# Another order of seven products, an earlier absolute value, and later loads in one stage of an attention and feed-forward kernel

## The chip, the core and the metric

The kernel runs on one core of a Trainium2 chip. A core has five engines with a queue of instructions each: TensorE (PE, with its weight loads shown apart as PEld), VectorE (DVE), ScalarE (ACT), GpSimd (POOL) and SyncE (SP, which here only issues DMA transfers). They run side by side and wait for each other through semaphores. The metric is the device time of one execution in microseconds; times shown are medians of several runs. Positions in the profile are microseconds from the first instruction.

## The reference

Attention with normalised queries and keys is followed by a feed-forward block with a squared ReLU:

```python
# q, k, v: (8, 12, 448, 64); w_in: (768, 2048); w_out: (2048, 768)
def attn(q, k, v, g_q, g_k):
    def rmsnorm(x, g):
        return x / np.sqrt(np.mean(x * x, axis=-1, keepdims=True) + 1e-06) * g
    scores = np.matmul(rmsnorm(q, g_q), rmsnorm(k, g_k).transpose(0, 1, 3, 2)) / 8
    attn = np.exp(scores - np.max(scores, axis=-1, keepdims=True))
    attn = attn / (np.sum(attn, axis=-1, keepdims=True) + 1e-09)
    return np.matmul(attn, v)
# x: the attention's result as (8 * 448, 12 * 64)
h = np.maximum(x @ w_in, 0.0)
out = (h * h) @ w_out
```

q, k, v and the result are float32; the weights w_in and w_out arrive as float64 and are turned into float32 on the chip.

## The kernel before, in words

**Stages.** The eight batches are taken two at a time: four spans of 896 rows. A pair is two heads of one batch; a batch has six pairs, so pairs 0 to 11 belong to span 0, and `NAT` is 12. The kernel first does the attention of span 0 alone (`attention_alone`). Then, for each span, comes the first product with w_in (`first_product`), and then the second product with w_out, whose matmuls are mixed with the attention of the next span. The last span's second product is `last_product`.

**Seven products.** Each matrix product is split into two halves in each direction, and the four block products are made from seven, in the manner of Strassen and Winograd: A11, S2, S1, S3, A12, A22 and S4. The letters name the weight side, for instance A11 a quarter of the weights and S1 a sum of two quarters. The row side has matching matrices: the quarters of x in `xT`, and their differences T1, T2, T3 and T4 in `xC` and `xT`. In `first_product` there are 8 columns `f` of seven products each, so 56 in all; a product is three float32 matmuls of 128 x 128 by 128 x 448, each shown as two records in the profile. The weight side of a product is a tile `sw` of 192 KB, loaded by SP with `load_blocks` from a scratch tensor `w1s` in DRAM. There are five such tiles in turn: a load waits until PE has left the tile of five products ago.

**Banks.** A product is summed in a PSUM bank: A11 and A12 in `pa`, S2 in `pb`, S1 and S4 in `pc`, S3 and A22 in `pd`. The second product in a bank goes on summing onto the first, and may start only once the first has been read: ACT copies A11 to `p1`, and A12 goes on in `pa`; DVE makes `z = p1 + pb`, then `y = z + pc`, and S4 goes on in `pc`; DVE adds `y` and `pd`, and A22 goes on in `pd`. The quarters of the result are then activated by ACT as Relu and Square (in place, L1063 and L1065 of before). `pb`, `pc` and `pd` come from `bank`, which takes two banks, m and n, in turn; `pa` comes from other banks. In the first column of span 0, `order_of` gives the order A11, A12, S2, S1, S3, A22, S4; in all others it is A11, S2, S1, S3, A12, A22, S4.

**Weights.** The float64 weights are turned into float32 while span 0 runs. There are 32 rows of blocks, first 16 of w_in, then 16 of w_out; a row takes one `tick` of four steps in `prepare`, and `weights(upto)` advances the steps. Step 1 has a clamp of the exponents on DVE (L603), step 2 an integer conversion on ACT (L606) and a shift on DVE (L608), step 3 a bit merge on DVE (L613) and, for rows from 13 on, the final integer sum (L579, on DVE) for the row before. The first instruction for a row is the Abs on ACT (`unsigned`, L589), which step 4 issues for the row that comes next, so that step 1 can use it. For each pair of rows, POOL makes four sums (L583), and SP writes the blocks to `w1s` or `w2s`. Rows up to 12 are prepared during `attention_alone`; the rest during the first product of span 0, some 1.76 steps after each product. `u` counts the products from 0.

**What sets the order.** Each engine's queue is the order in which the program issues the instructions; it is written out by hand, and there is no scheduler. [...] At the end of `attention_alone`, for pair 11, SP is given `load(14)` (eight transfers of q and k, into the place where pair 12 lies) and `load_v(12)` (four transfers). The pair 12 is used in the attention that follows this first product; its `transposes` and the `squares` of pair 14 are issued after product 52.

Of the kernel before, what the change touches and what calls it, by code (L numbers as in the profile page):

```python
# [10 lines left out]
F32 = mybir.dt.float32  # L11
U32 = mybir.dt.uint32
AF = mybir.ActivationFunctionType
ALU = mybir.AluOpType
# [373 lines left out]
def attention_then_ffn_bounded(  # L388
# [162 lines left out]
    def prepare(t):  # L551

        def there(n):
            return 0 <= n < 2 * NFC

        def parts(n):
            low, high = pairs_of(words_of(n))
            return exponents_of(n), exponents_of(n).bitcast(U32), low, high  # L560

        def value(n, half):
            if not there(n):
                return

            to = ((A11, A12), (A21, A22)) if n < NFC else ((A11, A21), (A12, A22))
            places = [place_of(n, k) for k in to[n % 2]]
            part = slice(half * HW, (half + 1) * HW)
            if not doubles:
                nc.gpsimd.tensor_copy(blocks_of(n)[:, places[half]], words_of(n).bitcast(F32)[:, part])  # L570
                return
            _, eu, low, _ = parts(n)
            if n < EARLY // 4:
                dst = blocks_of(n)[:, places[half]]
                nc.gpsimd.tensor_tensor(*[x.bitcast(I32) for x in (dst, low[:, part], eu[:, part])], ALU.add)
            elif half == 0:
                dst = blocks_of(n)[:, places[0]:places[1] + 1:places[1] - places[0]]
                low, eu = (x.rearrange("p (h m) -> p h m", h=2) for x in (low, eu))
                nc.vector.tensor_tensor(*[x.bitcast(I32) for x in (dst, low, eu)], ALU.add)  # L579

        def total(n, dst, x, y, op):
            if there(n) and n % 2:
                nc.gpsimd.tensor_tensor(*[blocks_of(n)[:, place_of(n, i)] for i in (dst, x, y)], op)  # L583

        def unsigned(n):

            if there(n) and doubles:
                e, _, _, high = parts(n)
                nc.scalar.activation(e, high.bitcast(F32), AF.Abs)  # L589

        if t == 0:
            unsigned(0)
        n = t - 3
        if there(n) and n % 2:
            c = n % NFC // 2
            dst = w1s[c] if n < NFC else w2s[:, c // 4, :, c % 4]
            first = place_of(n, A11)
            nc.sync.dma_start(dst.rearrange("k p m -> p k m"), blocks_of(n)[:, first:first + 7])
            written[0] = n + 1
        if there(t) and doubles:  # L600
            e, eu, low, high = parts(t)

            nc.vector.tensor_scalar(e, e, 2.0 ** -15, 1.875 * 2.0 ** 16, ALU.max, ALU.min)  # L603
        yield
        if there(t) and doubles:
            nc.scalar.activation(low.bitcast(I32), low, AF.Copy, scale=2.0 ** -29)  # L606
            bits = banks.get("bits", eu)
            nc.vector.tensor_scalar(bits, eu, 3, 0x3FFFFFF8, ALU.logical_shift_left, ALU.bitwise_and)  # L608
        if t < 3:
            load_words(t, t - 1)  # L610
        yield
        if there(t) and doubles:
            nc.vector.scalar_tensor_tensor(eu, high, 0xC0000000, bits, ALU.bitwise_and, ALU.bitwise_or)  # L613
        total(t - 2, S3, A11, A21, ALU.subtract)
        total(t - 2, S4, A12, S2, ALU.subtract)
        value(t - 1, 0)
        yield
        unsigned(t + 1)
        value(t - 1, 1)
        total(t - 1, S1, A21, A22, ALU.add)  # L620
        total(t - 1, S2, S1, A11, ALU.subtract)
        load_words(t, t - 1)
        yield
# [17 lines left out]

    def order_of(span, f):

        return (A11, A12, S2, S1, S3, A22, S4) if span == f == 0 else range(7)

    N1 = HF * 7
    FIRST = (5,5,5)
# [288 lines left out]
    def attention_alone():  # L936


        for i in range(NAT):
            more = i + 1 < NAT  # L940
            if 0 < i < NAT - 3:
                load(i + 3)
            scores(i, 0)
            scores(i, 1)
            if i == 0:

                transpose(1, 1, 1)
                scores(0, 2)
                scores(0, 3)
                transpose(1, 0, 0)  # L950
                add_up(0, 1)
                norm(2)
                load_v(1)
                values(0, (0, 1))
                load(3)
                yield
                continue
            if more:
                transpose(i + 1, 1, 0)
            values(i - 1, (2, 3))  # L960
            add_up(i, 1)
            if i + 2 < NAT:
                norm(i + 2)
            elif not more:
                norm(NAT)
                load(NAT + 2)
            yield
            if more:
                transpose(i + 1, 0, 0)
            load_v(i + 1)  # L970
            if i + 2 < NAT:
                roots(i + 2)
            yield
            scores(i, 2)
            scores(i, 3)
            total_of(i - 1)
            values(i, (0, 1))
            finish(i - 1)
            yield
            if added(i) == 3:  # L980
                add_up(i, 2)
            combine_x(i - 1)
            if NAT <= i + 3 < NAT + 2:
                load(i + 3)
            yield
        values(i, (2, 3))
        total_of(i)
        finish(i)
        combine_x(i)
# [67 lines left out]
    def first_product(work, span):  # L1057
# [10 lines left out]

        for f in range(HF):
            n = begins[span, 1] + f * 7  # L1070
            order = order_of(span, f)
            g11, g12 = gT[:, f, 0:S], gT[:, f, S:2 * S]
            g21, g22 = gT[:, HF + f, 0:S], gT[:, HF + f, S:2 * S]
            add = nc.vector.tensor_tensor
            ps_of = {}
            for at, i in enumerate(order):

                into, rhs = {A11: ("pa", B11), S2: ("pb", T2), S1: ("pc", T1), S3: ("pd", T3),
                             A12: ("pa", B21), A22: ("pd", T4), S4: ("pc", B22)}[i]
                first = into not in ps_of  # L1080
                if first and into == "pa":
                    if span == 0 and f:
                        ps_of[into] = ps_o.tile([P, S], F32, tag="ot"[f % 2], name="pa")
                    else:
                        ps_of[into] = ps_s.tile([P, 2, 512], F32, tag="s", name="pa")[:, 0, 0:S]
                elif first:
                    ps_of[into] = bank(into)
                ps = ps_of[into]
                load_blocks(n + at + 5)
                for c in range(HC):  # L1090
                    nc.tensor.matmul(ps, stream[n + at][:, c], rhs[:, c], start=first and c == 0,  # L1091
                                     stop=c == HC - 1, skip_group_check=not first)
                if i == A11:
                    p1 = work.tile([P, S], F32, tag="p1", name="p1", bufs=1)
                    nc.scalar.copy(p1, ps)  # L1095
                elif i == S2:
                    z = work.tile([P, S], F32, tag="z", name="z")
                    add(z, p1, ps, ALU.add)  # L1098
                elif i == S1:
                    y = work.tile([P, S], F32, tag="y", name="y")  # L1100
                    add(y, z, ps, ALU.add)
                elif i == A12:
                    activate(g11, ps)
                else:
                    g, x = {S3: (g22, y), A22: (g21, z), S4: (g12, z)}[i]
                    add(g, x, ps, ALU.add)  # L1106
                    activate(g, g)
                if span and f and i in (S1, A22):
                    combine(f - 1, (int(i == A22),))
                if span and f == HF - 1 and i == S4 and span + 1 < NSPAN:  # L1110
                    combine(f)
                yield
# [359 lines left out]
    with tc.tile_pool(name="words", bufs=2) as spare["pool"]:  # L1472
# [20 lines left out]
        with tc.tile_pool(name="first_product", bufs=2, reuse_waits="tile") as work:  # L1493
            for u, _ in enumerate(first_product(work, 0)):
                if u == 6:

                    left = ps_s.tile([P, 2, 512], F32, tag="s", name="bits")
                    banks["bits"] = left.rearrange("p a b -> p (a b)")[:, 0:NW].bitcast(U32)
                weights(min(ALL, EARLY + (ALL - EARLY) * (u - 1) // (N1 - 6)))
                if u == N1 - 5:  # L1500
                    norm(NAT + 1)
                if u == N1 - 4:
                    transposes(NAT)
                    squares(NAT + 2)
# [124 lines left out]
```

## Time and profile before

| what | us |
|---|---|
| median of three runs | 1347.29 (1347.04 to 1348.31) |
| the profiled execution, in all | 1347.79 |
| its span, first to last instruction | 1346.0 |
| PE busy | 1324.7 |
| attention alone | 0 to 133.14 |
| first product of span 0 | 133.14 to 263.94 |
| the rest | 263.94 to 1346.0 |

The granted clock of TensorE was 0.999 of full speed. In the profile, `L1091` is line 1091 of the kernel before. A row "A <- B" of the waits says that A's engine stood still until B released it, with the total time, the number of times and the longest. A row of the timeline gives start, length, engine, line and operation, what it writes and reads, and in brackets the idle time ahead of it. The chain that ended last follows the last instruction back through whatever released each step.

### The profile page before, as it was taken

Reading aid. Unit: us, or ns where it says so; the run is one execution under the profiler, and the core shown is the slowest. Engines: PE = TensorE matmul, PEld = TensorE weight load, DVE = VectorE, ACT = ScalarE, POOL = GpSimd, SP = SyncE. Lnnn points to the kernel's source line nnn. Section 1 sums busy time; section 2 is a strip of 40 time slices with the busy share of each in tenths; the row PEclk is TensorE's granted clock in tenths of the full one; section 3 lists DMA queues with packets and bytes.
Section 4 is the critical chain, followed back from the end, with each engine's and each line's share of the span. In section 5 each row is a group of like instructions: output and inputs, shape, how many; then the busy total and the mean of one; then the engine's idle time right before and its main releaser. Section 6 shows DMA issues by size and latency. Waiting matters only on the chain.

```text
span 1346.0 us, 17761 instructions
## 1 busy us (share of the span) xinstructions
PE 1324.7 (98%) x5930; PEld 698.9 (52%) x5930; DVE 861.9 (64%) x1333; ACT 486.4 (36%) x939; POOL 681.0 (51%) x546
## 2 busy tenths in 40 slices
PE   8999999999999999999999999999999999999997
PEld 3333444444445655444444755444444665556887
DVE  6999788489988233467888533457888823336553
ACT  7886466555541011345553011235554101111000
POOL 5766533466765222647774522447676522322452
PEclk9999999999999999999999999999999999999999
DMA  8977999666665433346755433345664444421333
GB/s 226 244 214 200 312 357 331 187 131 121 138 140 125 104 88 88 102 105 132 149 125 144 110 90 88 92 113 117 134 129 128 107 100 139 131 88 47 115 103 56
DMA packets 413817, 190.18 MB, mean 141 GB/s; under 512 B 282388, under 2 KB 408724, under 8 KB 413716
## 3 DMA queue, kind: packets, MB, share of 16 engines
q1 hardware_dynamic: 406164, 180.21, 51.8%
q0 software_dynamic: 4736, 8.40, 2.5%
q8 instruction: 49, 0.80, 0.3%
q10 hardware_dynamic: 2816, 0.34, 0.2%
q14 instruction: 52, 0.43, 0.1%
HBM read 155.72 MB, written 33.16 MB: 140 GB/s over the span
## 4 chain that ended last, share of the span: by engine, by line
PE 87%; DVE 7%; ACT 4%; issue 1%; DMA 1%; POOL 0%; SPq 0%; DVEq 0%; ACTq 0%
PE ps L1190 21%; PE pd L1091 11%; PE pa L1091 10%; PE pc L1091 10%; PE sc L796 7%; PE pav L878 7%; PE pb L1091 5%; PE ps L1373 3%; PE ps L1241 2%; PE pd L1345 2%; PE pc L1345 2%; PE pa L1345 2%; ACT gT L808 2%; PE pd L1175 1%; PE pc L1175 1%
## 5 line engine op out<-in xcount | busy, mean ns | idle before, releaser
L1067 POOL TENSOR_TENSOR gT<-gT 128x448 f32<-128x448 f32 x96 | 94.2, 983 | 258.0 <-ACT gT L1063 258.0
L761 POOL TENSOR_TENSOR half<-half,mhalf 128x28 f32<-128x28 f32 x36 | 184.1, 5115 | 70.2 <-DVE half L760 56.2
L1190 PE MATMUL ps<-gT,sw 128*128 128x448 f32 x432 | 169.3, 545 | 0.0
L1063 ACT ACTIVATE gT<-gT 128x448 f32<-128x448 f32 x96 | 55.4, 577 | 300.5 <-DVE gT L1106 300.5
L1091 PE MATMUL pa<-xT,sw 128*128 128x448 f32 x384 | 155.0, 540 | 0.6 <-ACT p L1095 0.6
L1190 PEld LDWEIGHTS ps<-gT,sw 128*128 128x128 f32 x432 | 80.1, 190 | 87.2 <-issue 85.2
L1190 PE MATMUL ps<-gC,sw 128*128 128x448 f32 x288 | 113.1, 546 | 0.0
L796 PE MATMUL sc<-qkT 64*64 64x448 f32 (+1 forms) x1152 | 110.1, 497 | 0.3 <-ACT pr L798 0.2
L1091 PEld LDWEIGHTS pa<-xT,sw 128*128 128x128 f32 x384 | 72.7, 190 | 71.8 <-issue 70.5
L583 POOL TENSOR_TENSOR gC<-gC 128x384 f32<-128x384 f32 x64 | 76.4, 1213 | 63.4 <-DVE gC L579 61.7
L1190 PEld LDWEIGHTS ps<-gC,sw 128*128 128x128 f32 x288 | 53.2, 190 | 59.5 <-issue 57.7
L846 POOL DMA_DIRECT2D xT<-factors x72 | 38.1, 534 | 89.9 <-DMA factors<-square 65.2
L1106 DVE TENSOR_TENSOR gT<-z,pd 128x448 f32<-128x448 f32 x32 | 19.8, 620 | 97.8 <-PE pd L1091 97.8
L798 ACT ACTIVATE pr<-sc 128x896 f32<-128x896 f32 x87 | 76.9, 909 | 11.1 <-PE sc L796 11.1
L1091 PE MATMUL pd<-xT,sw 128*128 128x448 f32 x192 | 77.9, 542 | 1.5 <-DVE z L1098 1.4
L763 POOL TENSOR_TENSOR qk<-qk,half 128x448 f32<-128x448 f32 x72 | 76.9, 1089 | 2.8
L1091 PE MATMUL pd<-xC,sw 128*128 128x448 f32 x192 | 77.5, 540 | 0.7 <-DVE gT L1106 0.7
L1091 PE MATMUL pb<-xC,sw 128*128 128x448 f32 x192 | 77.5, 540 | 0.2 <-DVE gT L1106 0.2
L1091 PE MATMUL pc<-xT,sw 128*128 128x448 f32 x192 | 77.5, 540 | 0.0
L1091 PE MATMUL pc<-xC,sw 128*128 128x448 f32 x192 | 77.4, 539 | 0.0
L878 PE MATMUL rest<-pr,vt 64*64 64x448 f32 x348 | 72.7, 537 | 0.0
L878 PE MATMUL pav<-pr,vt 64*64 64x448 f32 x348 | 72.7, 537 | 0.0
(282 smaller groups left out, 2455.1 us busy)
## 6 DMA issues: line engine op xcount, KB each, us to landing
sw<-w1s SPq DMA_DIRECT2D x224, 192.0 KB, 2.4
sw<-w2s SPq DMA_DIRECT2D x102, 256.0 KB, 3.5
w1s<-gC SPq DMA_DIRECT2D x8, 1344.0 KB, 6.9
w2s<-gC SPq DMA_DIRECT2D x8, 1344.0 KB, 6.8
qk<-in_q_dram SPq DMA_DIRECT2D x144, 56.0 KB, 2.6
qk<-in_k_dram SPq DMA_DIRECT2D x144, 56.0 KB, 2.4
xT<-factors POOLq DMA_DIRECT2D x72, 112.0 KB, 3.4
vt<-in_v_dram SPq DMA_DIRECT2D x72, 96.0 KB, 3.8
```

Source lines behind the costliest of these rows:

```text
L583: nc.gpsimd.tensor_tensor(*[blocks_of(n)[:, place_of(n, i)] for i in (dst, x, y)], op)
L761: nc.gpsimd.tensor_tensor(half, half, mhalf, ALU.pow)
L763: nc.gpsimd.tensor_tensor(qkn[:, s], raw[:, s], half[:, s * NG:(s + 1) * NG].rearrange("p g -> p g ()").to_broadcast([P, NG, 32]), ALU.mult)
L796: nc.tensor.matmul(sc[part, h, 0:n], qkT[rows, 0, 1, keys], qkT[rows, 0, 0, of], start=True, stop=True)
L798: nc.scalar.activation(pr, sc[:, :, 0:n], AF.Exp)
L878: nc.tensor.matmul(into, vs[i][rows, h, c, :], probs[i, c][rows, h, :], start=(c == 0), stop=(c == NF), skip_group_check=True)
L1063: nc.scalar.activation(g, src, AF.Relu)
L1067: nc.gpsimd.tensor_tensor(g, g, g, ALU.mult)
L1091: nc.tensor.matmul(ps, stream[n + at][:, c], rhs[:, c], start=first and c == 0, stop=c == HC - 1, skip_group_check=not first)
L1190: nc.tensor.matmul(ps, stream[n][:, c % 4], rhs_of[i][:, c], start=c == 0, stop=c == HF - 1)
L1345: nc.tensor.matmul(ps, lhs[:, c], rhs[:, c], start=first and c == 0, stop=c == HK - 1, skip_group_check=not first)
L1373: nc.tensor.matmul(ps, weights_of(o, m, c // HK)[:, c % HK], rhs_of[i][:, c, part], start=c == 0, stop=c == HF - 1)
```

## The change

Three things change, all in or around the first product of span 0.

1. The first column of span 0 takes the products in the order A11, S1, A12, S2, S3, S4, A22. `y` is made as soon as both `pb` and `pc` are there. In this column, `pb` takes the bank that held the even pairs' values, `pc` is bank m and `pd` bank n; one extra turn keeps the alternation of the later columns as it was.
2. The Abs of the next row is issued in step 3, before its end, instead of step 4, for ticks from 13 on.
3. `load(14)` and `load_v(12)` leave the end of `attention_alone` and are issued, the v first, after product 40 of the first product.

```diff
         value(t - 1, 0)
+        if t >= EARLY // 4:
+            unsigned(t + 1)
         yield
-        unsigned(t + 1)
+        if t < EARLY // 4:
+            unsigned(t + 1)
         value(t - 1, 1)
...
-        return (A11, A12, S2, S1, S3, A22, S4) if span == f == 0 else range(7)
+        return (A11, S1, A12, S2, S3, S4, A22) if span == f == 0 else range(7)
...
                 norm(NAT)
-                load(NAT + 2)
...
-            load_v(i + 1)
+            if more:
+                load_v(i + 1)
...
             n = begins[span, 1] + f * 7
+            turn[0] += span == f == 0
...
+                elif first and span == f == 0:
+                    ps_of[into] = (ps_o.tile([P, S], F32, tag="o", name="pb") if into == "pb"
+                                   else bank(into, int(into == "pd")))
                 elif first:
                     ps_of[into] = bank(into)
...
-                elif i == S2:
-                    z = work.tile([P, S], F32, tag="z", name="z")
-                    add(z, p1, ps, ALU.add)
-                elif i == S1:
-                    y = work.tile([P, S], F32, tag="y", name="y")
-                    add(y, z, ps, ALU.add)
+                elif i in (S2, S1):
+                    if i == S2:
+                        z = work.tile([P, S], F32, tag="z", name="z")
+                        add(z, p1, ps, ALU.add)
+                    if "pb" in ps_of and "pc" in ps_of:
+                        y = work.tile([P, S], F32, tag="y", name="y")
+                        add(y, z, ps_of["pc"], ALU.add)
...
                 weights(min(ALL, EARLY + (ALL - EARLY) * (u - 1) // (N1 - 6)))
+                if u == 5 * N1 // 7:
+                    load_v(NAT)
+                    load(NAT + 2)
```

## The prediction

> **What bounds the kernel now.** I read the page first: the busy times and the engines' shares of the chain that ended last.
>
> ```profile
> PE 1324.7 (98%) x5930; PEld 698.9 (52%) x5930; DVE 861.9 (64%) x1333; ACT 486.4 (36%) x939; POOL 681.0 (51%) x546
> PE 87%; DVE 7%; ACT 4%; issue 1%; DMA 1%; POOL 0%; SPq 0%; DVEq 0%; ACTq 0%
> ```
>
> PE is the bound, idle for 1346.0 - 1324.7 = 21.3 us. Only idle time of PE in the stage that the change touches can be won. The view by stretches (attention alone, span 0's first product, the rest) puts it in size:
>
> ```profile
> 0.00:133.14 133.14, 124.06 (x611) 47.89 (x611) 115.84 (x179) 104.15 (x186) 86.41 (x70) 1.00 0.82 224
> 133.14:263.94 130.80, 127.95 (x341) 63.29 (x344) 97.47 (x127) 71.53 (x114) 57.98 (x53) 1.00 0.88 302
> 263.94:1346.00 1082.06, 1072.66 (x4984) 587.72 (x4984) 648.61 (x1027) 310.73 (x639) 536.57 (x425) 1.00 0.47 112
> ```
>
> The columns are length, busy time of PE, PEld, DVE, ACT and POOL, clock, DMA share, GB/s. The middle stage is the one changed: PE idles 2.85 us, and its DMA share is 0.88. PE's timeline there has one row per product of six matmul records:
>
> ```profile
> 133.14 2.52 PE L1091 MATMUL pa<-xT,sw 128*128 128x448 f32 x6
> 136.28 2.52 PE L1091 MATMUL pa<-xT,sw 128*128 128x448 f32 x6 [0.62 <-ACT p L1095]
> ...
> 146.28 2.52 PE L1091 MATMUL pd<-xC,sw 128*128 128x448 f32 x6 [0.71 <-DVE gT L1106]
> ...
> 169.26 2.52 PE L1091 MATMUL pb<-xC,sw 128*128 128x448 f32 x6 [0.16 <-DVE gT L1106]
> ...
> 191.35 2.52 PE L1091 MATMUL pd<-xT,sw 128*128 128x448 f32 x6 [1.35 <-DVE z L1098]
> ...
> 261.52 2.42 PE L1091 MATMUL pc<-xT,sw 128*128 128x448 f32 x6
> ```
>
> Undisturbed products start every 2.2555 us (138.64, 140.90, 143.15). Fifty-five such steps are 124.05 us, but the first and last starts lie 128.38 us apart: 4.33 us are lost, the refill of about 0.1 us after each stall included. By starts: 0.99 at product 1, 0.98 at product 5, 0.42 at 15, 0.17 at 18, 1.62 at 24, 0.15 at 41. The waits of this stretch say what makes DVE late:
>
> ```profile
> DVE gC L603 <- ACT gC L589: 14.1, 8, 2.1
> PEld pc L1091 <- DMA sw<-w1s: 0.6, 1, 0.6
> ```
>
> L589 is the Abs of a row. DVE's timeline shows the wait ahead of the 1.35 us stall:
>
> ```profile
> 184.28 0.61 DVE L1106 TENSOR_TENSOR gT<-z,pc 128x448 f32<-128x448 f32 x1
> 186.94 0.97 DVE L603 TENSOR_SCALAR gC<-gC 128x768 f32<-128x768 f32 x1 [2.05 <-ACT gC L589]
> ...
> 190.68 0.61 DVE L1098 TENSOR_TENSOR z<-p,pb 128x448 f32<-128x448 f32 x1
> ```
>
> After its addition of 184.28, DVE sits 2.05 us, because ACT first does Relu and Square of that sum and only then the Abs. SyncE's timeline at the stage's start shows the transfers that move:
>
> ```profile
> 133.88 1.89 SPq L688 DMA_DIRECT2D qk<-in_q_dram  x4
> 135.87 2.00 SPq L688 DMA_DIRECT2D qk<-in_k_dram  x4
> 137.91 0.48 SPq L543 DMA_DIRECT2D gT<-in_moe_w_out_dram  x1
> 138.48 0.92 SPq L705 DMA_DIRECT2D vt<-in_v_dram  x2
> 139.44 1.33 SPq L707 DMA_DIRECT2D vt<-in_v_dram  x2
> ```
>
> **What the skill says.** The Trainium skill, "TensorE: Matmul & The Clock Gate" (opening table), gives ScalarE, VectorE and GpSimd strict first-in-first-out queues; the 2.05 us above is such a queue. "DMA: Bandwidth & Descriptors" (Anatomy of one DMA) says a DMA's semaphore wait happens on the issuing sequencer; the trace agrees, as the loads above begin only when POOL's scaling of pair 12 is done, and the weight tiles wait behind them until 140.87. The same page (Specifications) wants 512 B or more per piece for full rate; q and k go in packets of 128 B, and DMA shows 0.35, 0.69 and 0.96 busy at only 57 to 111 GB/s over 134 to 140 us. "SBUF — State Buffer" (Who interferes with whom) says a DVE operation with two SBUF inputs contends with GpSimd; xC's subtractions took 1.30 us beside POOL and 0.62 without.
>
> **The change part by part.** No instruction is added or taken away; they are only reordered.
>
> *Order of products.* Product k would start at 133.14 + 2.2555k. Product 1 is now S1 into bank pc: its operand T1 is many microseconds old, so nothing waits, and the copy of A11 (135.70 to 136.24) hides under it; A12 at 137.65 finds it done. A product is released 2.46 us after its start (143.15 to 145.61). S2 starts at 139.90; its operand's last part was ready at 138.5. Then DVE: z at 142.4 to 143.0, y (which now needs z) to about 143.8; S4, which adds onto the bank that y reads, starts at 144.42, margin 0.6. S3 is released at 144.62. DVE has two row operations first (0.55 + 0.96), so the sum of S3 ends near 145.8; A22 needs that bank at 146.67, margin 0.9. Thus both stalls go: -1.97 us. If DVE were later by more than these margins, the excess comes back one for one.
>
> *Banks.* Column 1's pb and pc now wait for S4's and A22's sums, two and three products old, where pb had one product's time before. Afterwards the alternation is the same. Zero.
>
> *Abs one step earlier.* In ACT's order each Abs now stands ahead of Relu and Square, which wait for DVE. Its own waits, for a row's words and for POOL's value sums of four rows back, ended earlier (POOL's last is at 143.94). Its 0.9 us delays one Relu; readers of that are a stage away. It frees up to 14.1 us of DVE. At product 15: the sum of A22 can start at its release, 133.14 + 12 x 2.2555 + 2.46 = 162.67; the four operations to the end of S4's sum took 165.34 to 169.20, so 166.53, against 166.97 when product 15 wants the bank: margin 0.44. At product 24: A22's sum at 178.45, S4's sum begins 3.27 later (181.01 to 184.28), row work 0.53 after, z ends 4.36 after that (186.94 to 191.30): 186.61 against 187.27, margin 0.66. Gain -0.42 - 0.17 - 1.62 = -2.2 us. The loss of 0.15 at product 41 is a weight tile behind a w2s write that waits for POOL, which waits for DVE; that goes too, while tile 18, behind such a write, may now cost about 0.1.
>
> *The loads moved.* At the start, four v and eight q/k issues leave the queue (3.99 + 2.29 = 6.28 us). A row of w_out and the weight tiles from 5 on go out when the product ahead frees their buffer. Nothing to win by itself, but tile 9, which took 8.9 us, gets room. The 12 issues now come after tile 44's, at product 39's release, 133.14 + 39 x 2.2555 + 2.46 = 223.6; 0.3 for tile 44, then 6.28: tile 45 issues at 230.2 and is wanted at 234.6. Landing took 2.3 at least, 5.2 in the median, 8.9 at most: 232.5 to 239.1. Next in the queue is a w2s write, then tile 46, wanted at 236.9 and likely landing at 235 to 237.5. Row 30's value sum on DVE waits for that write's landing (6.8 median: 237.5, against the 237.4 at which DVE gets there); behind it is the sum of S3, which A22 needs with some 0.4 to spare. So the cost lies between 0 and about 4 us. I take 0.7, as DMA was only 0.64 and 0.46 busy at 228 to 232 before. Squares of pair 14, which need the data, come twelve products later and are covered.
>
> Sum: -4.33 + 0.1 + 0.7 = -3.5 us. All later work follows the products and is PE-bound (0.20 and 0.31 are its longest PE gaps), so the gain stays. The profiled execution had 1346.0 us of span and 1347.79 in all; the median of the runs is 1347.29, so I forecast 1347.29 - 3.5 = 1343.8, with a span near 1342.5. A measurement of this kernel tells about 0.2% (2.7 us) from no change.
>
> **Rivals.**
> *A: all stalls go, with a small wait near product 45.* 1342.9 to 1344.6, chance 0.66.
> *B: only the new order pays.* DVE runs at 97.47 of 130.80 us, and the margins of 0.44 and 0.66 may be eaten by POOL's port, or words may come late; then the later stalls stay or tiles 45 and 46 eat 2 us: 1347.29 - 1.97 = 1345.3. Against it: eight Abs waits are gone for two margins that need one. Chance 0.21.
> *C: slower.* The 12 small transfers meet a busy DMA, each of the later ones waits for the eighth before it to land, and two rounds of 8.9 us pass: tile 45 issues at 241.7, lands near 245, and PE stands 10 us: 1347.29 - 4.3 + 10 = 1353. It decides once tile 45 lands 4.3 us after 234.6, at 239, and is measurable from 241.6. Against it: the same burst took 6.28 us before. Chance 0.11.
> *D: the moved Abs does nothing,* as ACT is still held by a wait in front of it: as B's time. Chance 0.02.
>
> **Numbers.** Predicted 1343.8 (A). The range 1342.6 to 1347.0 takes in A and B, the 4.33 us won in full, and half of the doubtful cost of the burst. Faster by over 0.2% (below 1344.6): 0.67; within: 0.22; slower: 0.11.
>
> **What would show it.** Right: products 1 and 5 start without idle time; DVE's row of waits on Abs falls from 14.1 to under 4 us; the last product starts near 258 instead of 261.52; the later stage keeps its 1082 us. Wrong: PE or its weight load waits on a weight tile or on a sum between 230 and 245 for more than 1 us; or DVE still late at products 15 and 24.

## The result and the profile after

The changed kernel took 1345.03 us in the median of 22 runs (1343.33 to 1346.61), the kernel before 1347.26 us in 22 runs beside them (1345.68 to 1349.32). The ratio is 0.9983, with a 95% interval of 0.9977 to 0.9988: 2.2 us less, between 1.6 and 3.1. The profiled execution has a span of 1343.1 us instead of 1346.0.

The page's busy row and the three stretches of the kernel after (length, then busy time of PE, PEld, DVE, ACT and POOL, clock, DMA share, GB/s):

```profile
PE 1324.0 (99%) x5930; PEld 699.4 (52%) x5930; DVE 860.5 (64%) x1333; ACT 486.2 (36%) x939; POOL 681.1 (51%) x546
```

```profile
0.00:133.23 133.23, 124.38 (x610) 47.83 (x610) 116.50 (x179) 104.01 (x186) 86.23 (x70) 1.00 0.82 225
133.23:261.20 127.97, 127.25 (x337) 63.51 (x337) 98.74 (x127) 71.51 (x114) 57.62 (x52) 1.00 0.88 307
261.20:1343.10 1081.90, 1072.34 (x4985) 588.05 (x4984) 645.23 (x1027) 310.64 (x639) 537.22 (x426) 1.00 0.47 112
```

The changed stage is 127.97 us long instead of 130.80, and PE is idle in it for 0.72 us instead of 2.85. The other two stretches kept their length within 0.2 us. PE's timeline of the kernel after, one row per product:

```profile
135.59 2.42 PE L1098 MATMUL pc<-xC,sw 128*128 128x448 f32 x6
...
146.87 2.42 PE L1098 MATMUL pd<-xC,sw 128*128 128x448 f32 x6
...
167.16 2.42 PE L1098 MATMUL pb<-xC,sw 128*128 128x448 f32 x6
...
187.69 2.52 PE L1098 MATMUL pd<-xT,sw 128*128 128x448 f32 x6
...
226.44 2.52 PE L1098 MATMUL pc<-xT,sw 128*128 128x448 f32 x6 [0.15 <-DMA sw<-w1s]
...
238.48 2.49 PE L1098 MATMUL pa<-xT,sw 128*128 128x448 f32 x6 [0.50 <-DMA sw<-w1s]
...
258.85 2.42 PE L1098 MATMUL pc<-xT,sw 128*128 128x448 f32 x6
```

The rows shown are products 1, 6, 15, 24, 41, 46 and 55. Product 0 starts at 133.23; its 55 successors, at 2.2555 us each, would take 124.05 us, and they take 125.62. I call the difference the stage's loss: 1.57 us, where the kernel before lost 4.33. The stalls at products 1, 5, 15 and 18 are gone, but for 0.10 us at product 1, which every profile with the new order shows. What is left besides is 0.33 at product 24, 0.41 at 41 and 0.73 at 46. Two of these rows name weight tiles as the reason. In the kernel before no row of PE named one, but two of its small losses were waits for tiles as well: tile 18 landed at 176.09, and PE began product 18 at 176.23; tile 41 landed at 229.80, and PE began product 41 at 229.84. The waits of 130 to 265 us after:

```profile
DVE gC L603 <- ACT gC L589: 0.7, 2, 0.3
...
PEld pc L1098 <- DMA sw<-w1s: 0.9, 1, 0.9
...
PE pa L1098 <- DMA sw<-w1s: 0.5, 1, 0.5
```

DVE's wait on Abs fell from 14.1 us to 0.7.

### The profile page after: what moved, and what is told of

Read it like the earlier page. It is cut to its first block, busy times and chain, and to the rows that moved or that the text cites. A ratio compares the mean times of both kernels' runs of the same rounds, so it can differ in the third digit from the quotient of the medians.

```text
span 1343.1 us, 17769 instructions
## 1 busy us (share of the span) xinstructions
PE 1324.0 (99%) x5930; PEld 699.4 (52%) x5930; DVE 860.5 (64%) x1333; ACT 486.2 (36%) x939; POOL 681.1 (51%) x546
## 4 chain that ended last, share of the span: by engine, by line
PE 86%; DVE 7%; ACT 3%; DMA 3%; issue 1%; POOL 0%; SPq 0%; DVEq 0%; ACTq 0%; POOLq 0%
PE ps L1198 21%; PE pd L1098 10%; PE pa L1098 10%; PE pc L1098 10%; PE sc L799 7%; PE pav L881 7%; PE pb L1098 5%; PE ps L1381 3%; PE ps L1249 2%; PE pd L1353 2%; PE pc L1353 2%; PE pa L1353 2%; PE pd L1183 1%; PE pc L1183 1%; DMA sw<-w1s 1%
```

## The experiments

The table has every combination of the three parts, and the later variants. The loss is from one profile each; the ratio of the times to the kernel before has its 95% interval.

| kernel | stage's loss, us | where most of it is (product: us) | ratio |
|---|---|---|---|
| before | 4.33, again 4.30 | 1: 0.99, 5: 0.98, 24: 1.62 | 1 |
| e1 order | 3.56 | 9: 1.03, 15: 0.76, 24: 1.61 | 0.9994 (0.9986 to 1.0003) |
| e2 Abs | 2.72 | 1: 0.99, 5: 0.97, 18: 0.43 | 0.9991 (0.9984 to 0.9997) |
| e3 loads | 6.10 | 1, 5: 1.97, 18: 0.59, 24: 1.61, 46: 1.51 | 1.0015 (1.0007 to 1.0023) |
| e5 order, Abs | 0.87 | 9: 0.46, 24: 0.33 | 0.9982 (0.9975 to 0.9989) |
| e6 order, loads | 5.51 | 10: 0.80, 15: 1.07, 24: 1.62, 46: 1.94 | 1.0007 (0.9998 to 1.0016) |
| e10 Abs, loads | 3.71 | 1, 5: 1.97, 41: 0.41, 46: 0.74 | no interval |
| all three | 1.57, again 1.63 (e8) | 24: 0.33, 41: 0.41 and 0, 46: 0.73 and 1.22 | 0.9983; e8 0.9982 (0.9974 to 0.9990) |
| e4, e9 all, loads spread | 0.68, again 1.12 | 9: 0.26 and 0, 24: 0.33, 41: 0 and 0.71 | 0.9976 (0.9967 to 0.9985); e9 0.9976 (0.9965 to 0.9986) |

### e1: the new order alone

```diff
-        return (A11, A12, S2, S1, S3, A22, S4) if span == f == 0 else range(7)
+        return (A11, S1, A12, S2, S3, S4, A22) if span == f == 0 else range(7)
```

with the banks and `y` as in the change.

> The kernel before with the new order of products in span 0's first column alone; Abs and loads stay as before. Theory (the parts are separate): products 1 and 5 lose nothing (1.97 us back), products 15, 18 and 24 still lose about 2.2 us because DVE still waits about 14 us for Abs; first to last product start 126.4 us instead of 128.4, time 2 us lower. Rival (DVE paces the stage, so that what PE wins early it gives back at products 15 and 24): products 15 and 24 lose about 4 us, first to last stays near 128.4 and the time is within 0.5 us of before.

First to last took 127.61 us: between the two, and the time can't be told from that of the kernel before. Products 1 and 5 lose only the 0.10 us named above, and the waits on Abs stayed (14.0 us). But a new stall ate half of the gain, at product 9:

```profile
154.45 2.49 PE L1095 MATMUL pc<-xC,sw 128*128 128x448 f32 x6 [0.79 <-DMA sw<-w1s]
```

Its weight tile was issued at 144.60 and landed at 154.32, 9.7 us later. A weight row (143.10) and a w1s write of 1344 KB (143.58) were issued just ahead of it. With the early stalls gone, product 9 also comes sooner after that issue: its turn was 8.9 us later, where the kernel before had 9.8. (A product's turn is the start of the product before it plus 2.2555 us.) The theory that each part stands alone fell with this run. DVE as the pace of the stage could explain only the growth of product 15's loss from 0.42 to 0.76.

### e2: the earlier Abs alone

```diff
+        if t >= EARLY // 4:
+            unsigned(t + 1)
         yield
-        unsigned(t + 1)
+        if t < EARLY // 4:
+            unsigned(t + 1)
```

> The kernel before with the Abs one step earlier alone. Theory: DVE's wait on Abs falls from 14.1 us to under 3, products 15, 18 and 24 lose about 0.4 us together instead of 2.2, products 1 and 5 still lose 1.97; first to last near 126.5 us, time 1.8 us lower. Rival (the order is needed for the Abs to come in time): DVE keeps over 8 us of waits on Abs and first to last stays over 127.5 us.

```profile
DVE gC L603 <- ACT gC L589: 0.7, 2, 0.3
```

First to last took 126.77 us, and the ratio of 0.9991 is 1.2 us. Product 15 lost nothing and product 24 lost 0.33. Product 18 lost 0.43, but not because of DVE: its weight tile landed 8.69 us after its issue, and PE waited for it. The two are more than the 0.4 expected for them together. The Abs comes in time without the new order; the rival fell.

### e3: the moved loads alone

```diff
                 norm(NAT)
-                load(NAT + 2)
...
-            load_v(i + 1)
+            if more:
+                load_v(i + 1)
...
+                if u == 5 * N1 // 7:
+                    load_v(NAT)
+                    load(NAT + 2)
```

> The kernel before with the load of pair 14's q and k and of pair 12's v moved to product 40 alone. Theory (the move costs and gives nothing by itself): a weight tile is late by about 0.7 us near product 46, the other losses stay at about 4.2 us; first to last near 129.0 us, time 0.5 to 0.8 us higher. Rival (the move gives: the weight tiles and rows at the stage's start come earlier and DVE is less late): products 15 to 24 lose 1 us less and the time is lower by 0.5 us or more.

```profile
242.67 2.49 PE L1091 MATMUL pa<-xT,sw 128*128 128x448 f32 x6 [1.28 <-DMA sw<-w1s]
```

The move is a loss of its own: 1.51 us at product 46 instead of 0.7, the stalls on DVE and ACT untouched, 0.59 us at product 18 for a late weight tile, the ratio 1.0015, about 2 us. In this kernel DVE's value sum of row 30 also stood 0.5 us for a w2s write to land.

### e5 and e6: two parts together, without loads and without Abs

Each is the changed kernel with one part put back: in e5 the loads of e3's diff, in e6 the Abs of e2's diff.

> The changed kernel with the twelve loads back at the end of the attention: order and Abs alone. Theory (in the order alone tile 9 came 0.95 us late because the burst of loads at 134 to 140 us pushed the weight rows and the w1s write together in front of it): product 9 is late again by 0.7 to 1.2 us, nothing is lost at product 46, and the stage loses 1.5 to 2.2 us in all (the changed kernel 1.57). Rival (tile 9's lateness came from DVE's lateness, through the w1s write): product 9 loses under 0.3 us and the stage under 1.1 us.

e5 lost 0.87 us in all. Product 9 was late by 0.46: between theory and rival, with the stage's loss on the rival's side. Whether DVE's lateness had a part in e1's 1.03 is not shown: the step from 1.03 to 0.46 is no larger than what tile 9's landing time moves by (7.6 to 8.9 us in the six profiles that have the new order and the loads moved). Nothing was lost at product 46. The stage loses 0.7 us less than the changed kernel does; the two ratios, 0.9982 and 0.9983, can't be told apart.

> The changed kernel with the Abs back in step 4: order and loads alone. Theory: product 9 is in time, products 15 and 24 lose about 2.2 us as DVE waits about 14 us for Abs, and product 46 loses about 1.4 us, as with the loads alone, since a late DVE makes the w2s write come in the middle of the burst; in all about 3.7 us and a time 0.5 us lower than before. Rival (0.7 us at product 46 are the burst's own, whatever DVE does): 0.7 us at product 46, in all about 3.0.

e6 was worse than both expected: 5.51 us. Product 9 was in time, as expected. With the new order, it lost 1.03 and 0.46 us where the loads stand at the start (e1, e5), and where they are moved it lost nothing in five of six profiles and 0.26 in e4; so moving the loads does ease that delay. But then the late DVE showed one product later, ahead of product 10:

```profile
153.36 0.95 DVE L603 TENSOR_SCALAR gC<-gC 128x768 f32<-128x768 f32 x1 [2.06 <-ACT gC L589]
```

```profile
155.88 2.52 PE L1095 MATMUL pd<-xT,sw 128*128 128x448 f32 x6 [0.53 <-DVE z L1103]
...
241.72 1.74 PE L1095 MATMUL pa<-xT,sw 128*128 128x448 f32 x4 [1.70 <-DMA sw<-w1s]
```

The last row is product 46, with 1.94 us lost. The two kernels with the loads in one burst and the late Abs (e3 and e6) lost 1.51 and 1.94 there, the ones with the early Abs 0.73, 1.22 and 0.74. The chain through product 46 has the tile from issue to landing, first in the changed kernel, then in e6:

```profile
232.16 6.18 DMA sw<-w1s
```

```profile
235.30 6.28 DMA sw<-w1s
```

In all five profiles with the burst the tile took about the same time, 6.15 to 6.28 us. What differs is how long before the product's turn it was issued: 5.7 us in the changed kernel and in e10, where the 0.41 us lost at product 41 had put off that turn, 5.2 in e8, 4.9 in e3 and 4.6 in e6. In e3 and e6 the burst took longer, since its first two transfers (v) held the queue for 1.35 and 1.65 us, and for 0.96 in the others. Why these two issues took longer is open.

### e10 and e11: the last combination, and the kernel before again

> The last of the eight combinations: Abs and loads without the new order. Theory (the burst costs 0.7 us in the stage when DVE is early and nearly 2 us when it is late): 1.97 us lost at products 1 and 5, about 0.4 at 18 and 24, 0.7 to 1.2 at product 46, in all 3.0 to 3.8 us. Rival (the burst's cost depends on the order of products instead): nearly 2 us at product 46, in all over 4.2 us.

e10, the kernel before with e2's and e3's diffs together, lost 3.71 us, 0.74 of it at product 46 and 0.41 at product 41: as the theory had it.

> The kernel before, profiled again, for how far a stage's loss moves from profile to profile: 4.1 to 4.6 us at the same products if the losses are fixed by the order of instructions; over 0.5 us away if they are chance.

e11 lost 4.30 us. The stalls on DVE and ACT repeat within 0.02 us. The stalls on weight tiles do not: product 18 lost 0.32 instead of 0.17, and product 41 nothing instead of 0.15. In the changed kernel and its repetition e8, product 41 lost 0.41 and 0, and product 46 lost 0.73 and 1.22. These two belong together, since a loss at product 41 puts off the turn of product 46: their sums are 1.14 and 1.22.

### e4, e8 and e9: the loads spread over three products

```diff
-                if u == 5 * N1 // 7:
+                if u == 39:
                     load_v(NAT)
-                    load(NAT + 2)
+                if u in (42, 46):
+                    load(NAT + 2, (u == 46,))
```

where `load` is given which of q and k it is to load.

> The changed kernel with the twelve loads issued in three groups of four, v after product 39, q after 42 and k after 46, instead of all twelve after product 40. Theory (SyncE's queue holds tile 45 and 46 back for the 6.7 us of the burst): the loss of 0.73 us at product 46 goes to under 0.1, first to last 0.6 us shorter than in the changed kernel (125.6), near 125.0 us. Rival (the w2s write ahead of tile 46 and a busy DMA delay it, not the queue): a loss of 0.4 us or more stays between products 42 and 50.

In the changed kernel, SyncE's queue around product 40 was this (start, length, line, what):

```profile
224.44 0.96 SPq L708 DMA_DIRECT2D vt<-in_v_dram  x2
...
226.82 2.16 SPq L691 DMA_DIRECT2D qk<-in_q_dram  x4
229.02 2.04 SPq L691 DMA_DIRECT2D qk<-in_k_dram  x4
...
231.69 0.38 SPq L598 DMA_DIRECT2D w2s<-gC  x1
232.16 3.92 SPq L672 DMA_DIRECT2D sw<-w1s  x4
```

The burst holds the queue from 224.44 to 231.06. The w2s write then goes out at 231.69, just ahead of tile 46 at 232.16, which lands at 238.35, while product 46 wanted it at 237.82. In e4 the write leaves earlier and the tile follows at 228.12:

```profile
225.03 1.18 SPq L672 DMA_DIRECT2D sw<-w1s  x2
226.76 0.37 SPq L598 DMA_DIRECT2D w2s<-gC  x1
228.12 0.32 SPq L672 DMA_DIRECT2D sw<-w1s  x1
```

```profile
236.95 2.42 PE L1099 MATMUL pa<-xT,sw 128*128 128x448 f32 x6
```

That is product 46, without a wait. First to last was 124.74 us, and product 46 lost nothing, neither here nor in the repetition e9. Its tile went out 8.8 us ahead of its turn, as it does in e5, which has no burst there, and not 5.7 us. So the burst in front of it was the cause of that loss. The w2s write stands just ahead of the tile in e4 as well, so the write alone does not make it late; what the write adds to the landing time was not tested (tile 45, issued before the write, landed after 2.9 us, and tile 46, behind it, after 6.2).

> The changed kernel as it is, beside the one with the spread loads. Theory: the stage loses 1.2 to 1.8 us, ratio to before near 0.9983.

> The spread loads again, beside the changed kernel. Theory: the stage loses 0.5 to 1.0 us, 0.7 us less than the changed kernel, and its ratio to before is 0.0004 to 0.0007 lower. Rival (the difference seen between them was chance): the same ratio within 0.0002.

Side by side, the changed kernel lost 1.63 us and the spread one 1.12 us, 0.71 of that at product 41 with a tile that took 9.0 us to land. That is 0.5 us less, where the theory had 0.7, and more than the 0.5 to 1.0 it gave the spread loads. The ratios are 0.9982 and 0.9976, so the spread one is 0.0006 lower; e4 had 0.9976 too. The intervals overlap, so its lead over the changed kernel is shown by the profile's product 46 and not by the times.

### e7: without POOL's sums beside DVE

```diff
-            if there(n) and n % 2:
+            if there(n) and n % 2 and n != 19:
```

in `total` of e4's kernel.

> The kernel with the spread loads, without POOL's four sums for the weight rows 18 and 19, whose blocks S1 to S4 are then left unset, so that the part of the result that uses them is not the reference's. Theory (DVE's value sum at 185.4 took 1.72 us instead of 0.95 because POOL's sums ran beside it): that sum takes 0.95 us again and product 24 loses nothing (0.33 us before). Rival (it was late for another reason): product 24 loses 0.2 us or more.

The changed kernel ahead of product 24, DVE and then POOL:

```profile
182.44 1.05 DVE L603 TENSOR_SCALAR gC<-gC 128x768 f32<-128x768 f32 x1
...
184.51 0.95 DVE L613 SCALAR_TENSOR_TENSOR gC<-gC,bits 128x768 uint32<-128x768 uint32 x1
185.39 1.72 DVE L579 CUSTOM_DVE_ANT_0 gC<-words,gC 128x1536 uint16<-128x1536 uint16 x1
187.03 0.61 DVE L1106 TENSOR_TENSOR z<-p,pb 128x448 f32<-128x448 f32 x1
```

```profile
182.07 4.22 POOL L583 TENSOR_TENSOR gC<-gC 128x384 f32<-128x384 f32 x4 [5.75 <-DVE gC L579]
```

and e7 (one run):

```profile
181.96 0.55 DVE L603 TENSOR_SCALAR gC<-gC 128x768 f32<-128x768 f32 x1
...
184.42 0.95 DVE L579 CUSTOM_DVE_ANT_0 gC<-words,gC 128x1536 uint16<-128x1536 uint16 x1
185.28 0.61 DVE L1107 TENSOR_TENSOR z<-p,pb 128x448 f32<-128x448 f32 x1
```

Without POOL's four sums the value sum takes 0.95 us again, z starts 52.52 us after product 0 instead of 53.80, and product 24 loses nothing. This confirms the theory, and shows that it was not the value sum alone: the clamp of L603 takes 0.55 us instead of 1.05. The two make up nearly all of the 1.28 us. In the kernel before the same POOL sums ran from 184.44 to 188.77, while DVE was waiting for Abs or in other operations, and the value sum came at 189.81, after them.

## Why the prediction was right, and where its sum was off

**Right: the order of products.** Products 1 to 8 run without a gap. The steps came where they were laid: z at 142.63, y from 143.28 to 143.90, the sum of S3 ending at 145.99, A22 at 146.87. Of the 1.97 us, the 0.10 at product 1 stays. What was laid as a separate gain is one only together with the other parts: alone it gave 0.77 us (e1), and 2.14 (3.71 to 1.57) when the other two are there.

**Right: the Abs.** The wait fell from 14.1 to 0.7 us, and S4's sum ahead of product 15 ended at 166.73, where 166.53 was laid, against a start at 167.16. This is the largest part: 1.61 us alone, and 3.94 us (5.51 to 1.57) when the other two are there.

**Right by luck: product 18.** The prediction put its 0.17 us to the Abs, though it also laid 0.1 for a late tile there. But product 18 waited for its weight tile, and it lost 0.17 to 0.59 us in all five profiles of the old order, with the early Abs too (0.43 in e2, 0.26 in e10), and nothing in the eight of the new order. So it is the order that ended this stall. How is open: the tile was issued 8.4 to 8.5 us ahead of its turn in all of them.

**Off: product 24.** The term read "z ends 4.36 after that", from a row in which DVE's value sum had POOL quiet beside it. With the wait gone, DVE reaches that sum inside POOL's stretch, and it takes 1.72 us instead of 0.95: z ended at 187.64, not 186.61. Of the 1.03 us between, 0.77 is the value sum, 0.08 the clamp (1.05 us instead of the 0.97 of the row that was used), and the rest, 0.19, moved product 24's turn as well. So a margin of 0.66 met 0.85 us that was not in the sum. The prediction quoted the sentence of the Trainium skill, "SBUF — State Buffer" (Who interferes with whom), that a DVE operation with two SBUF inputs contends with GpSimd, and named this as a threat to the margin, but put no number on it. Cost: 0.33 us, the refill of 0.10 included.

**Wrong: product 41.** "That goes too" did not hold: the changed kernel lost 0.41 us there. Tile 41 did go out earlier, 8.4 us ahead of its product's turn instead of 7.8, but it took 8.72 us to land, where it had taken 7.83. In e8 it was issued at the same place, landed after 8.07 us, and nothing was lost; in e9 it took 9.0 us and cost 0.71. What sets the landing time is not shown. In 11 of the 13 profiles the tile landed 0.3 to 0.6 us after the w2s write of 1344 KB that was issued just ahead of it.

**Right in mechanism, low in size: the loads.** The queue was held for 6.6 us, where 6.28 was laid; tile 45 issued at 231.16 (230.2 laid) and was in time; tile 46 behind the w2s write was late by 0.73, where the allowance for all was 0.7. That these two agree is luck: 0.7 was picked from a span of 0 to 4 us, and the loss at product 41 had put off the turn of product 46. Without it, e8 shows 1.22. One of the prediction's own signs of being wrong, a wait of PE or its weight load for more than 1 us between 230 and 245, was met by the weight load of product 46:

```profile
238.45 0.30 PEld L1098 LDWEIGHTS pa<-xT,sw 128*128 128x128 f32 x2 [1.19 <-issue]
```

The row says "issue", but the tile had landed only at 238.35; in e8 this wait was 1.67 us. "Nothing to win by itself" hid that the old place had a price too, tile 9, which came late once PE was faster (1.03 us in e1, 0.46 in e5). Still, the move cost more than it won in all four pairs of profiles that differ by it alone: 1.77 us (before and e3), 1.95 (e1 and e6), 0.99 (e2 and e10) and 0.70 (e5 and the changed kernel). The gain of the change comes from its other two parts; no run here shows a gain from the moved loads.

**The sum.** It left 0.8 us of the 4.33: 0.7 for the loads and 0.1 at product 18. The profile has 1.57: 0.10, 0.33, 0.41 and 0.73 at products 1, 24, 41 and 46. Of the stage's gain of 2.76 us the times show 2.2 (1.6 to 3.1). The time lies 1.2 us above the forecast of 1343.8, inside its range, but above the span given for rival A, and it is nearer to the 1345.3 of rival B, in which only the order pays. The time alone could not have told the two apart. The traces do: the order alone won 0.77 us and the Abs alone 1.61, and of the later stalls on DVE 0.33 us is left. Two of the reasons that B names, POOL beside DVE and a late tile 46, did cost time, but 0.33 and 0.73 us. The gain is 0.17%, and not the over 0.2% to which the prediction gave 0.67; with 22 runs of each kernel its interval still excludes no change. Rival C, a lasting wait behind the twelve transfers (1353), fell: in the changed kernel tile 45 landed at 234.03, and not after 239. Rival D fell with the 14.1 us of waits on Abs.

## What to carry to other kernels

When an engine gets rid of a wait, look at what it will now run beside: here the freed DVE met POOL's sums, and the faster PE met weight tiles that had been just in time. Price a burst of transfers by the queue time it takes and by what stands behind it in that queue; twelve issues in one piece cost PE 0.7 to 1.9 us at product 46, the same twelve in groups of four cost nothing there. Parts of a change that touch one pipeline must be tried in combination: the three parts' separate effects (-0.77, -1.61, +1.77 us) add up to -0.61, and together they gave -2.76. Try a change with each part left out, too: without the moved loads, this one lost 0.87 us in its stage instead of 1.57.

## What was not expected of the hardware

The landing time of one 192 KB weight tile ran from 2.2 us (e5) to 9.7 us (e1) within this stage, in which the DMA engines were busy for 0.88 of the time before and after. All the stalls on weight tiles in the 13 profiles fall on products 9, 18, 41 and 46, and each of these four tiles is the first to be issued behind a write of 1344 KB. Such a stall changed by up to 0.7 us from profile to profile (0 and 0.71 us at product 41 in e4 and e9), while stalls between engines repeated within 0.02 us. And a DVE operation that reads a single tile was slowed beside POOL as well: the clamp took 1.05 us instead of 0.55 (e7).
